# DiT block on one core: fc1's first twelve tiles once per batch instead of ten, and six more warm-up matmuls near the first transposes

## The chip, the cores and the metric

The kernel runs on one core of a Trainium2 chip. The metric is the time of one execution on the device in microseconds (us). Every run also lists the span, from the first to the last instruction, which is some 1.7 to 1.9 us shorter, and the mean granted clock of TensorE (PE), where 1.0 is the full rate. The mean clock leaves out the half rate of the start, before the clock's record begins (in the profile before at 6.27 us, where the spacing of the 128x512 warm-ups goes from 0.427 to 0.216 us; no_lead below lists 1.0 though its full rate came at 15.68 us), and it takes in the end, where PE has finished: the 0.999 of the profile before comes from the rate falling to 0.5 at 241.8 us.

## The reference

One transformer block of a diffusion model, in bf16, for x of shape (2, 256, 1152), two heads:

```python
mod = (_silu(c) @ w_mod).reshape(B, 6, 1, D)
shift_a, scale_a, gate_a, shift_m, scale_m, gate_m = [mod[:, i] for i in range(6)]
h = _layernorm(x) * (1 + scale_a) + shift_a
q, k, v = ...  # h @ wqkv
a = softmax(q k^T * Dh**-0.5) v @ wo
x = x + gate_a * a
h2 = _layernorm(x) * (1 + scale_m) + shift_m
m = _gelu(h2 @ w_fc1) @ w_fc2          # (1152 -> 4608 -> 1152)
return x + gate_m * m
```

## The kernel before

Two places matter. The first is the start. PE has nothing useful to do until x has been read and normalised, so the kernel multiplies zeros ("warm-ups", 128x512, four here and sixteen further on) until the first transposes of x can go. After those it computes the first part of `scale_a` from weights that a DMA brings, ACT adds one to it, the transposed x is scaled, and the k-projection's first steps run.

```python
def warm(n, dst):
    for _ in range(n):
        nc.tensor.matmul(dst[:], zeros[:, 0:P], zeros[:], start=True, stop=True)

warm(4, pwarm)
nc.tensor.transpose(pc[:], c_sb[:], ident[0:B * KD, 0:B * KD])
# ... cut ...
warm(16, pwarm)
# ... cut: statistics of x on DVE and ACT ...
pt_0 = transpose_x([0, 1], [0])        # waits for the normalised x (DVE)
# ... cut ...
scale_group(0)("a")                    # 18 matmuls on w_scale_a (DMA), then add one on ACT
for k in range(2):
    modulate(pt_0, k, k, 0, 0, P, "a")
pt_1 = transpose_x([0, 1], [1])
# ... cut ...
k_step(0, 0, P)                        # first matmuls of the k-projection
```

The second is fc1. Its input hT of batch 0 is ready earlier than that of batch 1, which is still on its way (layer norm, DMA transpose, modulate). So the first ten tiles of 128 features are computed twice with 256 columns, for batch 0 and then for batch 1, and the other 26 once with 512 columns.

```python
MSPLIT = 10
for b in range(B):
    for m0 in range(0, MSPLIT, 2):
        ms = range(m0, min(m0 + 2, MSPLIT))
        pacc = acc_tile([P, len(ms), N], "pacc")
        for m in ms:
            for k in range(KD):
                f1_mm(pacc[:, m - m0, :], m, k, b * N, (b + 1) * N)
        if b == 0 and ms[-1] == MSPLIT - 3:
            ln2_modulate(1)
        nc.scalar.activation(gT[:, ms[0]:ms[-1] + 1, b * N:(b + 1) * N], pacc[:], ACT.Gelu_apprx_tanh)
# ... cut ...
for m in range(MSPLIT, KF):
    pacc = acc_tile([P, T], "pacc")
    for k in range(KD):
        f1_mm(pacc[:], m, k, 0, T)
    nc.scalar.activation(gT[:, m, :], pacc[:], ACT.Gelu_apprx_tanh)
```

## Time and profile before

| | before |
|---|---|
| time at first, median of 3 | 244.39 us |
| with the 3 runs beside the changed kernel, median of 6 | 244.31 us (243.65 to 244.63) |
| span of the profiled execution | 242.3 us |
| PE busy | 235.4 us, 97% |
| PE waits of the start, after the first matmul | 0.7 + 0.4 + 0.3 us |

The fences below show chosen lines of each view, word for word; where a line is the last of the window that was asked for, its length and count end there. The head of the page of the kernel before: the span, each engine's busy time, then the busy share of PE in forty slices, in tenths.

```profile
span 242.3 us, 3983 instructions
PE 235.4 (97%) x1670; PEld 141.2 (58%) x1679; DVE 93.1 (38%) x207; ACT 70.8 (29%) x141; POOL 31.4 (13%) x47
PE   7899999999999999999999999999999999999994
```

Only the first two slices (12 us) and the last are not full. So PE is the bottleneck, and what PE loses at the start it loses for good, unless a hole further on takes it up. A line of the table of stretches of the kernel before (start and end, length, then busy us and instruction count of PE, PE's weight loads, DVE, ACT and POOL, then granted clock, DMA share, GB/s) shows how few holes there are after the start:

```profile
14.30:97.00 82.70, 82.49 (x679) 49.39 (x682) 47.29 (x109) 33.23 (x74) 13.96 (x19) 1.00 1.10 316
```

The list of waits of PE in the kernel before (who waited <- for whom: total us, times, longest):

```profile
PE pwarm L169 <- DVE eps_t L92: 1.2, 1, 1.2
PE pm L246 <- DMA w_scale_a<-in_w_mod_dram: 0.7, 1, 0.7
PE pt L264 <- ACT scale_a L256: 0.4, 1, 0.4
PE pt L264 <- ACT big L273: 0.3, 1, 0.3
PE pacc L779 <- ACT hT L665: 0.2, 1, 0.2
```

The timeline of PE at the start, kernel before (start, length, what, count; in brackets the idle time before it and who ended it):

```profile
3.23 5.11 PE L169 MATMUL pwarm<-zeros 128*128 128x512 bf16 x16
8.18 0.28 PE L264 MATMUL pt<-ident,xn 128*128 128x128 bf16 x2
9.14 0.60 PE L246 MATMUL pm<-sT,w_scale_a 128*128 128x2 bf16 x18 [0.69 <-DMA w_scale_a<-in_w_mod_dram]
10.09 0.27 PE L264 MATMUL pt<-ident,xn 128*128 128x128 bf16 x2 [0.35 <-ACT scale_a L256]
10.49 1.22 PE L286 MATMUL pk<-big,w_k 128*128 128x128 bf16 x19
```

And the timeline at fc1, kernel before:

```profile
97.75 1.18 PE L779 MATMUL pacc<-hT,w_f 128*128 128x256 bf16 x8
99.15 14.03 PE L779 MATMUL pacc<-hT,w_f 128*128 128x256 bf16 x127 [0.22 <-ACT hT L665]
107.01 1.58 ACT L665 ACTIVATE hT<-hT,shift_m,scale_m 128x256 bf16<-128x256 bf16 x3 [1.87 <-DMA hT<-xn]
107.02 1.63 DVE L669 TENSOR_SCALAR hT<-hT,scale_m,shift_m 128x256 bf16<-128x256 bf16 x6 [5.15 <-DMA hT<-xn]
```

PE starts fc1 at 97.75 us, stalls twice (0.53 us in all) for batch 0's last slices, and then runs through. It reaches batch 1 after 90 matmuls (five pairs of tiles at the 1.965 us a pair that the prediction takes from the trace), at 97.75 + 0.53 + 9.83 = 108.1 us, while batch 1's hT is modulated between 107.0 and 108.6 us. Its last slice is needed at 109.0: about 0.4 us to spare.

### The profile page before, as it was taken

The page shows a single profiled execution, that of the slowest core. Times are in us where ns is not written, and L with a number is a line of the kernel's source. Part 1 is how long each engine was busy: PE and PEld are TensorE (multiplying, and loading weights), DVE is VectorE, ACT ScalarE, POOL GpSimd, SP SyncE. Part 2 cuts the span into 40 slices and gives each one's busy share as a digit, 9 for nine tenths or more (in the row PEclk, how much of TensorE's full clock was granted, in tenths as well). Part 3 has the DMA queues.
Part 4 walks back from the last instruction along what each step waited for, and adds up shares of the span by engine and source line. Part 5 has one row for each costly group of instructions (what it writes and reads, how often), then busy time and mean ns, then how long its engine had stood idle before and what let it go on. Part 6 is the DMA issues. An engine that isn't in the chain of part 4 may idle for free.

```text
span 242.3 us, 3983 instructions
## 1 busy us (share of the span) xinstructions
PE 235.4 (97%) x1670; PEld 141.2 (58%) x1679; DVE 93.1 (38%) x207; ACT 70.8 (29%) x141; POOL 31.4 (13%) x47
## 2 busy tenths in 40 slices
PE   7899999999999999999999999999999999999994
PEld 2586454466666666888644444444665665666573
DVE  2762550765694676720000049997002000000001
ACT  6542250543736074863222233332000000000000
POOL 1012000000310616200000000001114111111111
PEclk9999999999999999999999999999999999999999
DMA  6999999999999997799999999996961000000000
GB/s 233 325 334 343 383 356 238 359 364 273 256 322 366 375 246 204 194 204 327 328 324 259 204 292 328 326 326 169 331 201 32 19 16 16 16 23 27 19 19 16
DMA packets 76989, 54.48 MB, mean 225 GB/s; under 512 B 26011, under 2 KB 72491, under 8 KB 76971
## 3 DMA queue, kind: packets, MB, share of 16 engines
q1 hardware_dynamic: 76240, 53.02, 77.8%
q0 software_dynamic: 704, 1.20, 1.5%
q8 instruction: 13, 0.21, 0.4%
q14 instruction: 5, 0.04, 0.0%
q10 hardware_dynamic: 27, 0.00, 0.0%
HBM read 46.90 MB, written 1.19 MB: 198 GB/s over the span
## 4 chain that ended last, share of the span: by engine, by line
PE 58%; ACT 2%; DMA 1%; issue 1%; DVE 0%; ACTq 0%; DVEq 0%
PE pacc L843 29%; PE pacc L779 29%; ACT hT L665 2%; DMA hT<-xn 1%; ACT xn L648 0%; ACT rstd L639 0%; DVE tmp L849 0%; DVE o_sb L851 0%; ACTq L665 0%; DVEq L849 0%
## 5 line engine op out<-in xcount | busy, mean ns | idle before, releaser
L779 PE MATMUL pacc<-hT,w_f 128*128 128x512 bf16 (+1 forms) x409 | 70.4, 332 | 0.5 <-ACT hT L665 0.2
L843 PE MATMUL pacc<-w_f,gT 128*128 128x384 bf16 (+2 forms) x468 | 70.5, 314 | 0.0
L843 PEld LDWEIGHTS <-gT 128*128 128x128 bf16 x468 | 44.4, 98 | 26.2
L779 PEld LDWEIGHTS <-w_f 128*128 128x128 bf16 x414 | 40.5, 98 | 29.9 <-issue 0.6
L467 DVE SCALAR_TENSOR_TENSOR late<-w_gate_mT,late 128x1152 bf16<-128x1152 bf16 x18 | 24.4, 1357 | 34.5 <-DMA w_gate_mT<-in_w_mod_dram 33.9
L849 DVE TENSOR_TENSOR tmp<-pacc,gate 128x384 f32<-128x384 f32 (+2 forms) x13 | 6.8, 526 | 64.3 <-PE pacc L843 51.0
L817 ACT ACTIVATE gT<-pacc 128x512 bf16<-128x512 f32 x26 | 15.5, 597 | 35.0 <-PE pacc L779 35.0
L467 DVE SCALAR_TENSOR_TENSOR s_spill<-w_scale_m,s_b 128x1152 bf16<-128x1152 bf16 x12 | 16.3, 1357 | 8.2 <-DMA w_scale_m<-in_w_mod_dram 7.9
L682 PE MATMUL pacc<-w_o,big 128*128 128x384 bf16 (+2 forms) x117 | 18.1, 314 | 0.0
L566 PE MATMUL pacc<-w_v,hT 128*128 128x384 bf16 x108 | 17.9, 326 | 0.0
L851 POOL TENSOR_TENSOR o_sb<-tmp,x 128x384 bf16<-128x384 f32 (+1 forms) x12 | 11.6, 973 | 47.8 <-DVE tmp L849 47.8
L682 PEld LDWEIGHTS <-big 128*128 128x128 bf16 x117 | 10.9, 98 | 7.0 <-ACT big L298 0.4
L566 PEld LDWEIGHTS <-hT 128*128 128x128 bf16 x108 | 10.4, 98 | 7.0 <-issue 0.2
L286 PE MATMUL pk<-big,w_k 128*128 128x128 bf16 (+2 forms) x100 | 13.3, 276 | 0.2
L688 POOL TENSOR_TENSOR x<-tmp,x_sb 128x384 f32<-128x384 f32 (+1 forms) x11 | 9.8, 890 | 18.0 <-DVE tmp L687 9.3
L493 PE MATMUL pacc<-hT,w_q 128*128 128x512 bf16 x53 | 11.8, 379 | 0.1
L324 POOL DMA_DIRECT2D gates_dram<-grow x4 | 2.0, 512 | 69.3 <-DVE grow L803 69.3
L286 PEld LDWEIGHTS <-w_k 128*128 128x128 bf16 x102 | 7.8, 97 | 3.1 <-issue 0.2
L493 PEld LDWEIGHTS <-w_q 128*128 128x128 bf16 x54 | 5.3, 97 | 6.4
L687 DVE TENSOR_TENSOR tmp<-pacc,gate 128x384 f32<-128x384 f32 (+2 forms) x13 | 6.7, 521 | 5.5 <-PE pacc L682 5.4
L505 ACT ACTIVATE big<-pacc 128x512 bf16<-128x512 f32 x9 | 4.8, 608 | 12.3 <-PE pacc L493 9.6
L169 PE MATMUL pwarm<-zeros 128*128 128x512 bf16 x20 | 7.0, 519 | 1.2 <-DVE eps_t L92 1.2
(98 smaller groups left out, 160.3 us busy)
## 6 DMA issues: line engine op xcount, KB each, us to landing
w_f<-in_w_fc_dram SPq DMA_DIRECT2D x14, 864.0 KB, 10.6
w_f<-in_w_fc_dram SPq DMA_DIRECT2D x2, 2592.0 KB, 12.0
w_f<-in_w_fc_dram SPq DMA_DIRECT2D x2, 1728.0 KB, 14.3
w_shift_a<-in_w_mod_dram SPq DMA_DIRECT2D x3, 864.0 KB, 10.6
w_v<-in_wqkv_dram SPq DMA_DIRECT2D x3, 864.0 KB, 6.0
w_gate_a<-in_w_mod_dram SPq DMA_DIRECT2D x3, 864.0 KB, 9.2
w_o<-in_wo_dram SPq DMA_DIRECT2D x3, 864.0 KB, 6.0
w_shift_m<-in_w_mod_dram SPq DMA_DIRECT2D x3, 864.0 KB, 13.0
```

The lines of the kernel that those rows point to most:

```text
L169: nc.tensor.matmul(dst[:], zeros[:, 0:P], zeros[:], start=True, stop=True)
L286: nc.tensor.matmul(pk[m][:, c0:c1], w_k[:, k, m * P:(m + 1) * P], hT0[:, k, c0:c1], start=(k == 0 and c0 == 0), stop=(k == KD - 1), skip_g ...
L467: nc.vector.scalar_tensor_tensor(spill, wT[:, j, :], 1.0, s_b[b], op0=ALU.mult, op1=ALU.mult, accum_out=dst(j, b),)
L493: nc.tensor.matmul(pq[m][:], w_q[:, k, m * P:(m + 1) * P], hT[:, k, :], start=(k == 0), stop=(k == KD - 1),)
L566: nc.tensor.matmul(pacc[:], hT[:, k, t * P:(t + 1) * P], w_v[:, k, pnl * PW:(pnl + 1) * PW], start=(k == 0), stop=(k == KD - 1),)
L682: nc.tensor.matmul(pacc[:], aT[:, k, t * P:(t + 1) * P], w_o[:, k, c0:c1], start=(k == 0), stop=(k == KD - 1),)
L688: (nc.vector if (t, i) in ((1, 2), (3, 3)) else nc.gpsimd).tensor_tensor(x1[:, t, c0:c1], tmp[:], x_sb[:, t, c0:c1], op=ALU.add)
L779: nc.tensor.matmul(dst, w_f1[m // KD][:, k, ml * P:(ml + 1) * P], hT[:, k, c0:c1], start=(k == 0), stop=(k == KD - 1),)
L817: nc.scalar.activation(gT[:, m, :], pacc[:], ACT.Gelu_apprx_tanh)
L843: nc.tensor.matmul(pacc[:], gT[:, kk, t * P:(t + 1) * P], w_f2[j][:, r, c0 - n * PW:c0 - n * PW + cw], start=(kk == 0), stop=(kk == KF - 1),)
L849: nc.vector.tensor_tensor(tmp[:], pacc[:], gate_m[:, b, c0:c0 + cw], op=ALU.mult)
L851: (nc.vector if last else nc.gpsimd).tensor_tensor(o_sb[:], tmp[:], x1[:, t, c0:c0 + cw], op=ALU.add)
```

## The change

Its intent: more batch 0 work in fc1 before batch 1's hT is needed; and PE kept at work in the lull around the first transposes.

```diff
-    warm(16, pwarm)
+    warm(18, pwarm)
     act_stats(ACT.Identity, dsum)
 ... cut ...
     pt_0 = transpose_x([0, 1], [0])
+    warm(3, pwarm)
     act_stats_finish()
 ... cut ...
     scale_group(0)("a")
     for k in range(2):
         modulate(pt_0, k, k, 0, 0, P, "a")
+    warm(1, pwarm)
     pt_1 = transpose_x([0, 1], [1])
 ... cut ...
-    MSPLIT = 10
+    MSPLIT = KD + CPP        # 12
```

## The prediction

> **What bounds the kernel now.** TensorE. The page gives it 235.4 of 242.3 us busy (97%), and the chain of waits ends in two PE groups, fc2 and fc1, 29% each. The table of stretches has PE busy 82.49 of 82.70 us between 14.3 and 97 us and 18.80 of 18.80 between 99.2 and 118. Holes: 1.2 us at the start, about 1.5 us net between 8.4 and 14.3 us (waits: 0.7 for the scale weights' DMA, 0.4 for the scale vector on ACT, 0.3 for ACT modulate), and about 0.5 us at 98.4 to 99.15, where fc1's first tile waits for ACT to modulate the last k-slices of batch 0. A PE delay before 14.3 us is therefore passed on to the end almost whole.
>
> **fc1 part.** Features 10 and 11 become 36 matmuls of 256 columns instead of 18 of 512. From the starts of successive GELUs a pair of half-width tiles takes 1.965 us, a full-width tile 1.942. Two tiles: 2 x 0.023 = +0.05 us. It buys 2 x 0.98 = 1.97 us more batch-0 work before batch 1's hT is needed. But in this trace nothing waits there: the modulates of batch 1 run 107.0 to 108.6 us, PE reaches batch 1 at about 108.1 and needs the slices at 0.109 us intervals, and the list of PE waits shows none. The modulate of batch 1 also moves one GELU back in ACT's order, harmlessly (that GELU's tile finishes before hT lands). So: insurance, gain about 0 in an undisturbed run. The 0.5 us wait at 98.4 us is for batch 0 and stays.
>
> **Warm-ups.** Six 128x512 matmuls on zeros. Their spacing is 0.427 us until 6.2 us and 0.216 us after. [...] no drop back is seen here: 128-column matmuls at 10.5 us start every 56 ns. So in this execution there is no low rate for the new matmuls to prevent.
> Cost at the warm rate: the two ahead move the first transposes from 8.18 to about 8.61 us. Three between end about 9.37, where the scale matmuls began at 9.14 (their DMA had just landed): +0.23 us, the rest of their time filling the hole that the DMA left. The one behind (0.22) fits in the 0.5 us in which PE waits for ACT's scale vector. The delay of 0.23 then passes through scale, modulate, k-steps, all ACT and PE in sequence. [...]
>
> **Sum.** +0.05 +0.25 = +0.3 us: 244.39 -> 244.7 us, range 244.0 to 245.4. Faster by over 2%: 1%; within 2%: 98%; slower by over 2%: 1%.
>
> **Right or wrong.** Right if the first scale matmul starts about 9.4 us rather than 9.14, the first k-step matmuls about 10.7 rather than 10.5, everything to fc1's start shifts by that, fc1's span grows 0.05 us, and no wait for hT of batch 1 appears in either. Wrong if the page's span shrinks with k-steps starting no later, or if batch 1 did wait in the timed executions.
>
> **What would make it wrong.** Executions of the kernel before that do fall back to half rate in the 8.4 to 14 us lull (about 1.5 us lost each), which the profiled one doesn't show; later landing of the batch-1 transposes in other executions (only about 0.4 us of slack); a different landing time of the scale weights, since anything later than 9.4 us hides the added warm-ups entirely.

## The result

| | before | changed |
|---|---|---|
| median of 6 runs | 244.31 us (243.65 to 244.63) | 244.14 us (244.0 to 244.5) |
| span of the profiled execution | 242.3 us | 242.5 us |

The ratio is 1.0001, with a 95% interval of 0.9984 to 1.0017: the same. A ratio here is the mean time of one kernel's runs over that of the other's of the same rounds, so it is not quite the ratio of the medians.

From the head of the page of the changed kernel:

```profile
span 242.5 us, 4040 instructions
PE 237.0 (98%) x1703; PEld 143.4 (59%) x1703; DVE 93.2 (38%) x207; ACT 70.7 (29%) x141; POOL 31.3 (13%) x47
```

PE is busier by 1.6 us and nothing is sooner: busy time that multiplies zeros is no progress. The PE waits of the changed kernel, after its first matmul:

```profile
PE pt L264 <- ACT big L273: 0.3, 1, 0.3
PE pacc L781 <- ACT hT L667: 0.2, 1, 0.2
```

The waits for the scale weights' DMA and for ACT's scale vector have gone from the list, since PE now multiplies zeros in them. The timeline of PE at the start, changed kernel, shows what that is worth:

```profile
3.14 5.54 PE L169 MATMUL pwarm<-zeros 128*128 128x512 bf16 x18
8.52 0.28 PE L264 MATMUL pt<-ident,xn 128*128 128x128 bf16 x2
8.63 0.81 PE L169 MATMUL pwarm<-zeros 128*128 128x512 bf16 x3
9.28 0.59 PE L246 MATMUL pm<-sT,w_scale_a 128*128 128x2 bf16 x18
9.73 0.38 PE L169 MATMUL pwarm<-zeros 128*128 128x512 bf16 x1
10.62 1.05 PE L286 MATMUL pk<-big,w_k 128*128 128x128 bf16 x16
```

The scale matmuls start 0.14 us later (9.28 against 9.14), the k-projection 0.13 us later (10.62 against 10.49). At fc1, changed kernel:

```profile
97.88 1.17 PE L781 MATMUL pacc<-hT,w_f 128*128 128x256 bf16 x8
99.27 13.91 PE L781 MATMUL pacc<-hT,w_f 128*128 128x256 bf16 x126 [0.22 <-ACT hT L667]
106.21 1.63 DVE L671 TENSOR_SCALAR hT<-hT,scale_m,shift_m 128x256 bf16<-128x256 bf16 x6 [4.21 <-DMA hT<-xn]
106.95 1.57 ACT L667 ACTIVATE hT<-hT,shift_m,scale_m 128x256 bf16<-128x256 bf16 x3
```

fc1 too begins 0.13 us later (97.88 against 97.75). The end of fc1 is read in the chain that ended last (start, length, what). Kernel before, then the changed kernel:

```profile
99.15 19.15 PE pacc L779 x173
...
168.59 70.30 PE pacc L843 x468
```

```profile
99.27 69.49 PE pacc L781 x424
168.76 70.31 PE pacc L845 x468
```

From 99.15 to 168.59 are 69.44 us, from 99.27 to 168.76 are 69.49: fc1 has grown by 0.05 us. So in these two executions the change costs 0.12 + 0.05 = 0.17 us, against a difference of 0.2 between the (rounded) spans. But the executions of either kernel differ by more than that, and the means show no cost. Either the parts are small costs lost in the scatter (theory A), or one of them gains something in executions other than the profiled ones (theory B).

### The profile page after: what moved, and what is told of

Same layout as the page of the kernel before. It is cut to its first block, busy times and chain, and to the rows that moved or that the text cites. A ratio compares the mean times of both kernels' runs of the same rounds, so it can differ in the third digit from the quotient of the medians.

```text
span 242.5 us, 4040 instructions
## 1 busy us (share of the span) xinstructions
PE 237.0 (98%) x1703; PEld 143.4 (59%) x1703; DVE 93.2 (38%) x207; ACT 70.7 (29%) x141; POOL 31.3 (13%) x47
## 4 chain that ended last, share of the span: by engine, by line
PE 58%; ACT 2%; DMA 1%; issue 0%; DVE 0%; ACTq 0%; DVEq 0%
PE pacc L845 29%; PE pacc L781 29%; ACT hT L667 2%; DMA hT<-xn 1%; ACT xn L650 0%; ACT rstd L641 0%; DVE tmp L851 0%; DVE o_sb L853 0%; ACTq L667 0%; DVEq L851 0%
## 5 line engine op out<-in xcount | busy, mean ns | idle before, releaser
L781 PE MATMUL pacc<-hT,w_f 128*128 128x256 bf16 (+1 forms) x432 | 70.7, 326 | 0.2 <-ACT hT L667 0.2
L781 PEld LDWEIGHTS <-w_f 128*128 128x128 bf16 x432 | 42.2, 98 | 28.2 <-issue 0.5
L819 ACT ACTIVATE gT<-pacc 128x512 bf16<-128x512 f32 x24 | 14.3, 597 | 32.3 <-PE pacc L781 32.3
L797 ACT ACTIVATE gT<-pacc 128x512 bf16<-128x512 f32 x12 | 6.9, 597 | 10.8 <-PE pacc L781 10.8
L169 PE MATMUL pwarm<-zeros 128*128 128x512 bf16 x26 | 8.6, 486 | 1.2 <-DVE eps_t L92 1.2
```

The costliest lines, as they stand in the source:

```text
L781: nc.tensor.matmul(dst, w_f1[m // KD][:, k, ml * P:(ml + 1) * P], hT[:, k, c0:c1], start=(k == 0), stop=(k == KD - 1),)
```

## The experiments

All kernels gave correct results. "Before" in the tables of runs is the kernel before, run again on the same chip in the same rounds, 11 executions each.

### Each part alone

```diff
# split_only: the kernel before with
-    MSPLIT = 10
+    MSPLIT = KD + CPP
# warm_only: the kernel before with
-    warm(16, pwarm)
+    warm(18, pwarm)
+    warm(3, pwarm)      # after pt_0
+    warm(1, pwarm)      # ahead of pt_1
```

> The kernel before with fc1's first twelve feature tiles once per batch, no new warm-ups. Theory A (both parts are small costs that no wait pays back): fc1 grows by 2 x 0.023 = 0.05 us, nothing else moves, ratio 1.000 (1.0002); first scale matmul at 9.14 us as before; no PE wait for the hT of batch 1. Theory B (the two parts have opposite signs and cancel; batch 1 does wait in the timed executions): this one is faster by 0.3 us or more, ratio 0.999 or below.

> The kernel before with the six new warm-ups, fc1 as before. Theory A: the first scale matmul starts at about 9.3 us, the first k-step matmul 0.13 us later than before (10.62 against 10.49), the shift arrives unchanged at fc1, ratio 1.0005. Theory B (the warm-ups keep some executions from falling back to the low clock): faster and with less scatter than the kernel before, the clock record of the kernel before showing low stretches after 7 us in some runs; ratio below 0.999. Theory B, other sign: slower by 0.3 us or more, against a gain of the fc1 part.

Measured: split_only 244.44 us (ratio 1.0001, 0.9986 to 1.0015), warm_only 244.16 us (0.9996, 0.9982 to 1.0011); before 244.33. split_only is not faster, so theory B in the form in which batch 1 waits in the timed executions is out. Beyond that the medians tell nothing; the single executions do. The mean granted clock of three of split_only's eight executions was 0.993, 0.992 and 0.984, with 244.70, 245.53 and 246.21 us; the other five were at 1.0 and 244.10 to 244.44 us. The kernel before had three of eleven at 0.993 (244.64 to 244.72). Of warm_only's six, none was below 0.998.

The profiled execution of split_only is one of the low ones. Its table of stretches, cut where its record of the granted clock changes:

```profile
7.70:11.11 3.41, 1.67 (x35) 1.49 (x36) 2.13 (x9) 1.40 (x6) 0.00 (x0) 1.00 1.12 331
11.11:14.52 3.41, 3.15 (x46) 3.09 (x44) 2.35 (x8) 1.54 (x6) 0.00 (x0) 0.50 1.12 321
14.52:17.93 3.41, 3.41 (x58) 3.24 (x57) 2.45 (x8) 1.10 (x3) 0.28 (x1) 1.00 1.09 340
```

From 11.11 to 14.52 us the clock (the column 1.00, 0.50, 1.00) was at half rate. One such stretch is 3.41 x 0.5 / 242.5 = 0.7% of the mean clock, which is the 0.993 (by the same sum, an estimate, 0.984 would be two such stretches and a little of the end). What had led to it shows in split_only's timeline:

```profile
7.20 0.28 PE L264 MATMUL pt<-ident,xn 128*128 128x128 bf16 x2
8.96 0.60 PE L246 MATMUL pm<-sT,w_scale_a 128*128 128x2 bf16 x18 [1.48 <-DMA w_scale_a<-in_w_mod_dram]
10.31 2.02 PE L286 MATMUL pk<-big,w_k 128*128 128x128 bf16 x24
98.32 0.84 PE L779 MATMUL pacc<-hT,w_f 128*128 128x256 bf16 x6
```

In this execution the full rate had come at 4.28 us, by the clock record, instead of the 6.27 us of the profile before. The first transposes, behind the sixteen warm-ups, were 0.98 us sooner (7.20 against 8.18), and PE stood idle for 1.5 us until the scale weights landed. So the half rate that the six warm-ups are to prevent does occur, here in an execution whose full rate came 2.0 us sooner than in the profile before. That is theory B's mechanism, and my reading of the profile before ("no low rate to prevent") held for that execution only. Not all of this execution's 245.53 us is the fall back: its stall for batch 0's hT at fc1 is 0.8 us longer than the changed kernel's (98.32 to 100.54 us against 97.88 to 99.27), and why hT came later is not shown.

warm_only's profiled execution shows the opposite case. The full rate came at 7.45 us, and the added warm-ups held up what waits behind them:

```profile
9.15 0.28 PE L264 MATMUL pt<-ident,xn 128*128 128x128 bf16 x2
9.26 0.81 PE L169 MATMUL pwarm<-zeros 128*128 128x512 bf16 x3
9.91 0.59 PE L246 MATMUL pm<-sT,w_scale_a 128*128 128x2 bf16 x18
```

The scale matmuls started at 9.91 us (9.3 was expected). In an execution with the sixteen old warm-ups and the full rate at 7.42 us (late_10 below) they started at 8.81:

```profile
8.81 0.60 PE L246 MATMUL pm<-sT,w_scale_a 128*128 128x2 bf16 x18
```

That is 1.1 us of cost, where the pair of first profiles shows 0.14. Of it, 0.45 us is the two in front (first transposes at 9.15 against 8.70) and 0.65 the three in between: in late_10 the scale matmuls follow the transposes at once, so there is no wait left for the three to fill.

### The suspected cost enlarged: ten warm-ups between

```diff
# between_ten: the kernel before with
     pt_0 = transpose_x([0, 1], [0])
+    warm(10, pwarm)
```

> The kernel before with ten warm-ups between the first transposes and the scale matmuls, none elsewhere. Theory A (a PE delay before 14 us reaches the end whole, because PE has no holes after that): ten matmuls at 0.216 us after 8.29 us move the scale matmuls from 9.14 to about 10.45, so +1.3 us at the first k-step, at fc1 and at the end: about 245.6 us, ratio 1.0054. Rival C (waits for DMA and ACT downstream absorb it, so the small measured cost is luck of slack, not of size): +0.6 us or less at the end, while the first scale matmul is still 1.3 us late.

Measured: 244.76 us, ratio 1.0026 (1.0006 to 1.0046), so +0.64 us by the ratio, half of what A said. In the profiled execution, whose full rate came at 7.14 us, the delay is there and passes on whole: the k-projection starts at 12.17 us (before: 10.49) and the span is 244.0 (before: 242.3), 1.7 us each.

```profile
12.17 0.49 PE L286 MATMUL pk<-big,w_k 128*128 128x128 bf16 x6
```

The other traces say the same: from the first matmul of the k-projection to the first of fc1 it is 87.26 us in the profiles before and changed, 87.27 here, and 87.25 to 87.30 in six more without a fall back (k_outer has 87.45), however early or late the k-projection starts. So rival C is wrong for that execution. Its six executions lie in two groups, four at 244.4 to 244.84 and two at 245.6 and 245.8 us. I take the lower group for executions whose full rate came early, in which most of the ten fill idle time; only one of the six has a trace, so this is argued, not shown. None of the six fell back.

### No leading warm-ups

```diff
# no_lead: the kernel before with
-    warm(16, pwarm)
+    warm(0, pwarm)
```

> The kernel before without its sixteen leading warm-ups (the four ahead of c's transpose stay). It asks what the array's clock does with the lull: if the clock follows recent activity, the full rate comes much later than 6.3 us, the first k-steps run at 107 ns per 128 columns instead of 56, and the kernel loses 1 to 4 us although the first transposes can start at 7.3 instead of 8.2 us. If the clock rises by itself some microseconds after the first matmul: full rate at about 6.3 us still, and no loss, ratio 1.000.

Measured: 244.83 us, ratio 1.0033 (1.0016 to 1.005), before 244.14. In the trace the full rate came at 15.68 us, and the first k-steps' 128-column matmuls started 107 ns apart instead of 56. So in this execution it did not rise by itself at 6.3 us: without the sixteen it came 8.2 us or more later than in the profiles with at least sixteen, where it came at 4.28 to 7.45 us. The loss, 0.8 us, is a little under the range I gave.

### How much slack batch 1 has

```diff
# split_8: the kernel before with
-    MSPLIT = 10
+    MSPLIT = 8
```

> The kernel before with only eight tiles once per batch instead of ten. Theory A (with ten, batch 1 is reached at 108.1 us with 0.4 us to spare, so no gain was to be had from twelve): PE now reaches batch 1 at about 106.1 us, before its hT (107.0 to 108.6 us), waits about 1.5 us (0.8 to 1.9, as the landing of the transposes varies), and the kernel takes +1.4 us, ratio 1.006. If the slack were much larger than I read, there is no wait and ratio 0.9998.

Measured: 246.38 us, ratio 1.008 (1.0064 to 1.0097). The wait is there, in split_8's timeline:

```profile
108.26 4.93 PE L779 MATMUL pacc<-hT,w_f 128*128 128x256 bf16 x39 [1.10 <-DVE hT L669]
```

Four of its six executions, the profiled one among them, also fell back to half rate at the start; the two that didn't took 245.61 and 246.15 us, 1.4 to 1.9 more than the kernel before in its executions of clock 0.996 and above (mean 244.22), where 1.4 was expected.

```diff
# late_10: the kernel before with, ahead of ln2_sqrt(3),
+    junk = act.tile([P, 896], BF16, name="junk")
+    for _ in range(2):
+        nc.scalar.activation(junk[:], x1[:, 2, 0:896], ACT.Identity)
# late_12: the same, and
-    MSPLIT = 10
+    MSPLIT = KD + CPP
# later_10, later_12: the same two with range(4)
```

> The kernel before (ten tiles once per batch) with two idle ACT passes over 896 columns ahead of the last row tile's square root, so that batch 1's hT comes about 1.9 us later (the outputs stay right). If the split is insurance with 0.4 us of slack at ten tiles: PE waits about 1.5 us (0.7 to 1.9) for batch 1's hT, ratio about 1.006. If ten tiles had far more slack: no wait, ratio 1.000.

> The same delay with twelve tiles once per batch. Insurance theory: 1.97 us more batch 0 work covers a delay of 1.9 us, so no wait or one under 0.4 us, ratio 1.000 to 1.001. If instead the ACT passes cost by another way than hT (late GELUs, PSUM buffers), this one is as slow as with ten tiles.

A miss of the instrument: late_10 took 244.1 us (ratio 1.0002), late_12 244.19 (1.0004). The passes delayed the last square root by 1.4 us (102.04 against 100.62), but batch 1's modulates still began at 107.1 us, as before: the transpose's DMA landed just as soon. So these two runs say nothing of the split. Four passes do:

> Ten tiles once per batch, with four idle ACT passes instead of two ahead of the last row tile's square root, as two did not move the landing of the last hT (107.1 us; it had come 3.4 us after its xn, where it took 5 us and more without the passes). Now xn is at about 105.6 us, so hT lands at about 109 and is modulated by 110.6 us: PE, which reaches batch 1 at about 108.0 us, waits 1.5 us or more: ratio about 1.007.

> The same four passes with twelve tiles once per batch. PE reaches batch 1 at about 110.0 us and needs the last slice at about 110.9: no wait or one under 0.3 us, ratio 1.000 to 1.001. If it is as slow as with ten tiles, the split is no insurance and the passes cost by another way.

Measured: later_10 246.33 us (ratio 1.0084, 1.0068 to 1.0099), later_12 244.38 (1.0012, 0.9997 to 1.0027). The PE waits at fc1, later_10 first, then later_12:

```profile
PE pacc L782 <- DVE hT L669: 1.2, 1, 1.2
PE pacc L782 <- ACT hT L665: 0.4, 2, 0.2
```

```profile
PE pacc L782 <- ACT hT L665: 0.4, 2, 0.2
```

The waits for ACT's hT are batch 0's, which every trace with the old slice order has. The wait for DVE's hT, batch 1's, is only in later_10. So the twelve tiles are insurance: 1.8 us worth of it where hT is late (1.0084 less 1.0012, of 244.2 us), and nothing where it is on time.

### The changed kernel again, for its single executions

> The changed kernel once more, unaltered, for its executions. So far 17 of 54 listed executions with the old warm-ups (the kernel before and the kernels that only touch fc1) show a mean granted clock of 0.993 or less, which is one stretch of about 3.4 us at half rate, and none of 18 with added warm-ups in the lull does. If the added warm-ups prevent the fall back (theory B's mechanism): none of this one's executions is below 0.996, some of the kernel before's are, and those are slower by 0.5 us or more. If it was chance: about one in three here too. Ratio 0.999 to 1.001 either way, since the fallback (0.3 x 0.6 us) and the later k-steps (0.1 to 0.7 us) about cancel.

Measured: 244.71 us, ratio 1.0015 (1.0 to 1.0031); before 244.23, a little above the 0.999 to 1.001 expected. In its profiled execution the full rate came at 7.03 us; the k-projection starts at 11.04 us and the span is 242.9, each 0.4 us later than in the changed kernel's first profile. None of its six executions was below 0.999; two of the kernel before's eleven were at 0.993 (244.62 and 244.67 us). All executions whose clock is listed, without no_lead, counted together:

| warm-ups | kernels | executions | of them below 0.996 |
|---|---|---|---|
| old | before | 33 | 6 |
| old | split_only, split_8, late_10, late_12, later_10, later_12, k_outer | 44 | 16 |
| with more in the lull | changed (12), warm_only, between_ten, k_outer_13_5 | 30 | 0 |

no_lead is left out because its record begins only at 15.68 us. The first two rows are the same program up to fc1, so their different rates are put down to chance. With the rate of the old ones (22 of 77), none in 30 would have a chance of 0.714 to the power of 30, about 4 in 100,000; with the rate of the kernel before alone (6 of 33), about 2 in 1,000. So, by count, the added warm-ups prevented the fall back in these executions; for the changed kernel's own 12 executions alone the count is too small (chance 0.09), and no trace has both an early full rate and added warm-ups.

What a fall back costs shows in the kernel before, all chips together: 6 executions with it average 244.70 us, 27 without it 244.14. The traces give it more directly: from the first matmul of the k-projection to the first of fc1 it is 88.01 us in each of the three with a fall back (10.31 to 98.32 in split_only), 0.75 more than the 87.26 of the others. And what the change costs: the changed kernel's 12 executions average 244.38 us, 0.24 above those 27. On the last chip alone it is more (244.57 against 244.15). Per execution, then, about +0.24 us against a saving of 0.56 us in 6 of 33, which is 0.10 us: a net cost of about 0.1 us, which neither a single set of runs nor all of them together resolve (the scatter leaves about 0.2 us on either side).

In the three traces with a fall back the full rate had lasted 6.82 to 6.83 us (4.28 to 11.11 us in split_only), twice the 3.41 us of split_only's half rate. So I compare the second 3.41 us after the full rate began, the last before the fall. All three traces with a fall back have the full rate early (split_only 4.28 us, later_10 4.38, split_8 4.70), and PE was busy 1.67, 2.04 and 1.79 us of that stretch. In the traces without one, the least full stretch of that kind near the start is 2.65 us, in late_12 (full rate at 5.15 us). Busy time does not tell them apart, though: at the end of later_10 a stretch with less, 1.56 us, kept the full rate. late_12 first, then later_10:

```profile
8.56:11.98 3.42, 2.65 (x46) 2.13 (x47) 2.45 (x10) 1.07 (x4) 0.00 (x0) 1.00 1.12 323
239.90:243.31 3.41, 1.56 (x28) 1.38 (x25) 0.66 (x3) 0.00 (x0) 0.72 (x1) 1.00 0.11 29
```

The columns that the matmuls stream were counted too, by the matmuls that start in a stretch (a 128x512 warm-up counts 512, a transpose 128, a scale matmul 2). The stretches before the three falls have 2,212 (split_only), 2,468 (split_8) and 2,980 (later_10), and the last 3.41 us before the fall at 241.8 us in the profile before has 768. Of the two stretches above that kept the full rate, later_10's end has 3,072 and late_12's has 3,620. These are counts of six stretches, in which some matmul records can be missing; what the clock goes by is not shown. The four warm-ups in the lull add 2,048 columns, which would bring split_only's stretch to about 4,260 (an estimate, 2,212 + 2,048), more than any of the four that ended in a fall.

### A version for both

The only PE wait left in fc1 is batch 0's. If the two tiles of a pair are computed in turn, slice by slice, each slice lasts twice as long and the late ones have time to come.

```diff
# k_outer: the kernel before with, for the first pair of each batch (m0 == 0),
-                for m in ms:
-                    for k in range(KD):
-                        f1_mm(pacc[:, m - m0, :], m, k, b * N, (b + 1) * N)
+                for k in range(KD):
+                    for m in ms:
+                        nc.tensor.matmul(
+                            pacc[:, m - m0, :], w_f1[0][:, k, m * P:(m + 1) * P], hT[:, k, b * N:(b + 1) * N],
+                            start=(k == 0 and m == m0), stop=(k == KD - 1), skip_group_check=True,
+                        )
# k_outer_13_5: k_outer with
-    warm(16, pwarm)
+    warm(13, pwarm)
+    warm(5, pwarm)      # after pt_0
+    warm(1, pwarm)      # ahead of pt_1
```

> The kernel before with the first pair of fc1 tiles of each batch accumulated k-slice by k-slice in turn (both tiles of a slice, then the next slice), so that PE needs a new hT slice every 0.22 us instead of 0.11. Theory A says that the only wait left in fc1 is batch 0's, 0.53 us at 98.4 to 99.15 us: with slices 6, 7, 8 ready at about 98.1, 98.6 and 99.1 us and needed at about 99.1, 99.3 and 99.5, it goes: -0.5 us, ratio 0.998. If what bounds it is something else there (the tail of wo, LDWEIGHTS at two matmuls per slice), no gain.

Measured: 243.65 us, ratio 0.9984 (0.9966 to 1.0002), before 244.14. The timeline of k_outer at fc1:

```profile
97.47 2.13 PE L793 MATMUL pacc<-hT,w_f 128*128 128x256 bf16 x18
99.43 8.02 PE L779 MATMUL pacc<-hT,w_f 128*128 128x256 bf16 x72
```

The eighteen matmuls take 99.43 - 97.47 = 1.96 us, the full rate of 0.109 us each: the stall is gone. From the first matmul of fc1 to the first of fc2 it is 70.15 us, 0.53 less than in the profile before (70.68); the ratio alone is not clear of 1. Three of its six executions still fell back (0.993, mean 244.15 us); the others took 243.29 to 243.37.

> The kernel before with fc1's first pairs accumulated slice by slice, thirteen leading warm-ups instead of sixteen, five between the first transposes and the scale matmuls and one behind those. If what the warm-ups cost is that they hold the scale matmuls up in executions where the full rate comes late, and what they save is the fall back where it comes early, then three fewer in front and five in the lull gets both: no execution below 0.996, first scale matmul at 9.3 us or earlier, and with 0.5 us from the slice order about 243.5 us, ratio 0.997. If only the slice order counts, 0.998, and some executions at 0.993 remain.

Measured: 243.55 us, ratio 0.9977 (0.9961 to 0.9992), before 244.23: faster, by about 0.6 us. No execution was below 0.999. In the profiled one the full rate came late, at 7.42 us:

```profile
8.25 1.24 PE L169 MATMUL pwarm<-zeros 128*128 128x512 bf16 x5
9.33 0.59 PE L246 MATMUL pm<-sT,w_scale_a 128*128 128x2 bf16 x18
```

The scale matmuls started at 9.33 us, where the eighteen-and-three of warm_only had them at 9.91 with the full rate at 7.45. So fewer in front and more in the lull cost less in this late case, and none of the six executions fell back. How much of the 0.0023 belongs to that and how much to the slice order stays open; k_outer alone had 0.9984 on another chip.

## Why the prediction was right

- **What bounds the kernel** was right. A delay at the start reaches the end whole: 0.13 us at the k-projection, 0.13 at fc1; in between_ten 1.7 us at both ends; and 87.25 to 87.30 us between the two points in nine traces.
- **fc1**: +0.05 us was predicted and 69.49 - 69.44 = 0.05 us measured. No wait for batch 1 in either trace, about 0.4 us of slack, and insurance only: confirmed by split_8 (slack used up, 1.1 us wait) and by later_10 against later_12.
- **Warm-ups, cost**: +0.25 us was the term (0.23 worked out). In the profiled pair it was 0.13 to 0.14. The 0.09 that is missing is not the warm-ups' doing: in the changed kernel's profile the leading ones began, and the full rate came, 0.09 us sooner (3.14 against 3.23, 6.18 against 6.27 us). Counted from there, the scale matmuls stand at 9.37 us, as forecast. Where the full rate came at 7.4 us the cost was 1.1 us (warm_only against late_10): the two in front cost 0.45 together, at the full rate, and the rest came from the three in between, which no longer had a wait to fill.
- **Warm-ups, gain**: here the argument was incomplete. "So in this execution there is no low rate for the new matmuls to prevent" was true of the one profile, but the sum gave the gain nothing in any execution. In 6 of 33 listed executions the kernel before does fall back. The prediction named this among what would make it wrong, and over-sized it at about 1.5 us lost; it was 0.75 us in the three traces from the k-projection on, and 0.56 us in the mean of executions. Two of the three traces also start the k-projection sooner (split_only 10.31 us, later_10 10.05, but split_8 10.60; before 10.49), which may be the difference; that is argued only.
- **The sum** of 244.7 us was 0.56 above the measured median of 244.14, within the range of 244.0 to 245.4. That range holds the kernel before's own 244.31 too, so the number tests little, and that a saved fall back offsets part of the cost was luck as far as the sum goes. The direction of +0.3 us is not resolved: by the ratios the two sets with the changed kernel gave +0.02 and +0.37 us.

## What to carry to other kernels

A single profile shows one way in which the array's clock came up (the full rate began at 4.28 to 7.45 us in the profiles with at least sixteen leading warm-ups); before saying that warm-up matmuls save nothing, or what they cost, look at the mean clock of every execution (it does not see the half rate of the start: no_lead lists 1.0 though its full rate came at 15.68 us) and at when the full rate began. Warm-ups ahead of real work were free here only while they filled a wait for something else (0.14 us of delay with the full rate at 6.2 us, 1.1 us at 7.4 us): put them into the gap after which the clock fell (1.5 us in split_only), and keep few in front of work that is ready. Splitting a stage by batch bought slack, not time (1.8 us where hT was late, nothing where it was on time), and where the first consumer of a late operand is short of it, interleaving two accumulations over its slices can take the wait away (0.53 us here).
